# One kernel, two orders of its steps: ScalarE asks for its pair of x first and for b1 last, and Wk's chunks 1 and 0 are turned ahead of the bias

## The chip, the core and the metric

The kernel runs on one core of a Trainium2 chip. The metric is device time in microseconds (us) for one execution, lower is better. The engines are TensorE (PE in the profile; PEld is its weight loads), VectorE (DVE), ScalarE (ACT), GpSimd (POOL) and SyncE (SP), which here only issues DMAs.

## What is computed

`x` is 2048 rows of 448 bf16 values. The output is `x + A(xn) + B(xn)`, with xn the row-normalised x.

```python
def _layernorm(x, axis=-1, eps=1e-5):
    m = jnp.mean(x, axis=axis, keepdims=True); v = jnp.var(x, axis=axis, keepdims=True)
    return (x - m) / jnp.sqrt(v + eps)
...
    # A: linear attention, H = 16 heads of 28
    qkv = (x @ wqkv) ...                       # q, k, v per head
    pq = einsum("bhsd,hdf->bhsf", q, w_phi);  pk = the same of k
    phi_q = concat([softmax(pq), softmax(-pq)]);  phi_k = the same of pk
    kv = einsum("bhsf,bhsd->bhfd", phi_k, v);  z = sum over s of phi_k
    o = einsum(phi_q, kv) / (einsum(phi_q, z) + 1e-6);  A = o @ wo
    # B: a feed-forward block, F = 1792
    h = x @ w1 + b1;  act = h * tanh(softplus(h))     # Mish
    B = act @ w2
```

## The kernel before

The 2048 rows are 16 tiles of 128; two tiles make a unit u (0 to 7). All work is cut into 300 named steps. The string ORDER names each once, and the program calls them in that order (run_order). Each call appends its instructions to the lists of the engines concerned (Program.op); waits are worked out from what each reads and writes. So ORDER sets the order within each engine's list and within each DMA queue, and nothing else: an engine goes through its list in order and waits where an input is late. ORDER also settles the PSUM banks: take1 and take2 hand out the bank or pair of banks (four pairs in all) that has been untouched for longest, at the time of the call. An instruction that opens a bank waits until the bank's last reader is done.

Names in ORDER, with the lines that the profile shows for their instructions. A last letter a, d, p, m or s says which engine does the evacuation or the issue: ScalarE, VectorE, GpSimd, a DMA transpose on SP, or SP.

- Loads. `lx1` to `lx6`: tiles of x (L275); `lkm`, `lvm`, `lkt`: Wk, Wv and their common last 64 rows (L278, L286); `lqT0` to 3: Wq turned by DMA (L290); `l1m0` to 2, `l1t`: W1's chunks and its last rows (L282, L286); `lp`: Wphi (L303); `lb`: b1 (L307); `l2`: W2 (L310); `lo`: Wo (four requests, L317). Those with `a` stand in ScalarE's own list.
- Filler. `zN`: N matmuls of 128x512 on constants (L381), that have no result anyone reads. `table`: ScalarE's table load (L320).
- GpSimd's constants. `pi` (identity and epsilon, L326 to L329), `pm` (mask, L334), `pw` (zeros of Wbd, L343), `pv` (ones beside v, L346), `pp0` to `pp4` (zero columns of buffers, L351), `pk` (mask2 and zeros of KVT, L355 to L364). `bd` makes the block-diagonal Wbd from Wphi (L549).
- Normalisation. `st<t>`: mean and variance of tile t, on VectorE (L472, L473) or on ScalarE (L464 to L468). `rs<u>`: the reciprocal root, on ScalarE (L485, L487), GpSimd (L478, L481) or, with t, ScalarE tile by tile. `xn<u>`: the normalised unit, on VectorE (L506) or GpSimd (L494, L501). `xt<u>`: its transpose, on TensorE with a copy (L514, then L519 on ScalarE or L521 on VectorE), or by DMA (L526).
- Weights of the features. `wtk<c>`: chunk c of Wk turned (L561); `wmk<c>`, `wmq<c>`: its product with Wbd, or that of Wq (L576); each has a copy on L519 or L521. `qd`: a copy within Wq turned (L294). `b1`: b1 turned (L679, copy L521).
- Per unit. `v`, `k`, `q` with u and part 1 or 2: two tiles' matmuls (L443), 8 and 6 of them, and after part 2 a copy of v, or two exponentials of k (L605) or q (L666) on ScalarE. `kn<u>.<s>`: sum and reciprocal on VectorE (L613, L615) and the scaling on GpSimd (L617). `e<t>`: tile t of exp(q) transposed by DMA into EqT (L674). `kv<u>`: the sum over rows (L634); `kvz` takes it to KVZ (L646 on VectorE, then a DMA transpose, L652).
- Feed-forward, first half. `f<q>.<fc>` part 1 and 2: half q of the rows, 128 columns fc of W1 (L443), then Mish on ScalarE into row fc of actT (L685).
- Output. `nd<t>`: numerator and denominator (L708), then six instructions on VectorE (L723 to L734); `ot<u>`: transpose of o by DMA (L743); `G<u>` parts 1 and 2: the second feed-forward product (L848), `g<t>` the same for one tile (L810); `wo<u>`: the product with Wo (L848 or L826). The last of them into a tile is followed by VectorE's addition (L775) and `sto`, `stt`, the store (L866, L863). `wob` copies 64 columns of Wo (L801, L802); `ep` makes a small constant on VectorE (L369, L372).

Buffers are shared. exp(q) of units 3 and 7 lies in row 4 of actT, units 2, 4 and 5 in rows 5, 3 and 2, and units 0, 1 and 6 in Eq0, where turned Wk lies before:

```python
    EQ_ROWS = (None, 4, 5, 3, 2)
    EQ_BUF = (0, 0, 2, 1, 3, 4, 0, 1)
```

Mish of f.4, f.5, f.3 and f.2 therefore waits until the `e` steps have read those rows, and the second user of a buffer waits for the `e` steps of the first. exp(k) of unit u lies in row 8+u.

Of the kernel before, what the change touches and what calls it, by code (L numbers as in the profile page):

```python
# [144 lines left out]


ORDER = """
lpa lx1a lba lvma lx3s lkms lkts lx2s lqT2 lqT1 lqT0 lqT3 lx6s lx0s lx4s table pw pp0 z10 st7d pm st3d st6a l1m1s pi
st2d bd b1 rs3a xn3d wtk2a wtk1a l1m2s wtk0d wmk2a rs1p xt3a pp2 xn1d wmk1a wtk3d wmk0a xt1d st4d wmk3a st5d pp4 v31a
v11d rs2t xn2d st15d v32a v12a k11 qd st14d wmq1a wmq2a xt2d rs7a xn7p wmq3a wmq0d k12 st12d st13d k31 st8d st9d k21 pp1  # L150
rs6p xt7m xn6d rs4p st0d xn4d k32 st11d pk q21 k22 q22 v21a pp3 q11 v22d xt6m ep q31 st10d rs5p xt4m q12 st1d q32 xn5d
rs0a l1m0s v71d pv xn0p k71 v72d xt5m k72 k61 e3 kn3.1 v61a k62 k41 v41a e2 kn2.1 v62a k42 q41 xt0m v42a q42 l1ts q51
v51d kn2.0 kn4.0 q52 e8 e9 kn4.1 kn3.0 q61 v52d q62 k51 e4 e5 kn1.0 kn1.1 kn6.0 k01 k52 kn5.1 f0.11 v01d k02 v02d e12
f1.01 f0.12 f1.31 f1.51 e13 f1.32 f1.02 e10 kn0.0 kn0.1 f1.52 e7 e11 f0.31 q71 f0.21 e6 f0.32 kn7.1 q01 f0.22 f0.131 q02
q72 kv4 kv1 kn6.1 e0 kv3 kv2 kv0 kn5.0 kv6 kv5 kn7.0 kv7 kvz f0.91 e14 f0.132 f1.101 e1 los f1.81 e15 f1.102 f1.82 f1.61
f0.92 wob f1.62 f0.121 nd0 l2a f1.11 f1.21 f1.12 nd1 f0.122 f1.22 f0.51 f0.41 ot0m f0.52 nd3 f1.71 f0.42 f1.72 f0.01
f1.131 nd2 f0.02 f0.61 f1.132 nd4 f0.62 f0.111 f0.81 f0.112 nd5 f0.82 f1.121 f0.101 ot2m nd12 ot1m f0.71 f1.122 f0.72
f0.102 f1.41 f1.111 f1.42 f1.112 nd6 G12 wo21 nd7 G11 nd13 wo11 ot3m f1.91 wo12 G02 nd10 G21 ot6m f1.92 nd11 G01 nd9
wo22 G22 wo61 nd8 G61 ot5m sto2 nd14 G41 G62 ot4m wo62 nd15 G42 wo51 wo31 wo41 wo01 ot7m G51 wo02 sto0 wo32 wo52 G31
wo42 G32 wo7F g14 wo7H G52 stt14 sto4 sto1 sto3 g15 sto5 sto6 stt15  # L160
"""


# [829 lines left out]
```

## Time and profile before

| | us |
|---|---|
| median of 3 runs (152.11 to 154.13) | 153.02 |
| the profiled execution, its own time | 151.93 |
| its span, first to last instruction | 150.2 |
| TensorE busy in it | 145.2 |
| VectorE, ScalarE, GpSimd busy | 101.9, 73.9, 40.4 |

All times of the trace count from the start of the span. A row of the timeline has the start, the duration, the engine (with a q: its sequencer, which issues DMAs and waits), the line of the kernel, the operation, what is written and read, the count of merged instructions and, in brackets, how long the engine sat idle before it and what ended that. The table by stretch gives each engine's busy time in each, then the granted clock of TensorE, the DMA share and GB/s. A row of a line's instructions gives count and shortest, median and longest duration in ns. The chain of waits gives start, length and what the end of the kernel was waiting for. A matmul's duration includes its way through the array, so that neighbours overlap; the steps from start to start show the rate.

### The profile page before, as it was taken

The numbers are of one execution on the slowest core, as the hardware profiler recorded it, in microseconds if no ns is written. First come the engines' busy times: TensorE is split into PE (matmuls) and PEld (weight loads), VectorE is DVE, ScalarE is ACT, GpSimd is POOL, SyncE is SP. The second block draws the span as 40 slices with busy tenths as digits, with TensorE's granted clock in tenths as the row PEclk, the third lists the DMA queues.
The fourth block names the chain that finished last, engine by engine and source line by source line (L and its number), as shares of the span: only waits on it lengthen the run. The fifth ranks groups of instructions, "written<-read, shape, count | busy, mean of one in ns | idle before, by whom it ended". The sixth has DMA issues, their size and how long they took to land.

```text
span 150.2 us, 4003 instructions
## 1 busy us (share of the span) xinstructions
PE 145.2 (97%) x1736; PEld 76.0 (51%) x1736; DVE 101.9 (68%) x227; ACT 73.9 (49%) x93; POOL 40.4 (27%) x58
## 2 busy tenths in 40 slices
PE   7799999999999999999979999999999999999993
PEld 2485555455544485454435445545555555554552
DVE  0788998999999803069759966897899755025231
ACT  2887999999899499848286485000200000000000
POOL 5330674599999990000000000000000000000000
PEclk9999999999999999999999999999999999999999
DMA  5999258496999904989900060033031300210054
GB/s 128 310 186 373 115 105 190 97 183 153 159 188 189 143 0 86 193 244 274 270 0 0 4 122 0 4 61 65 2 61 65 61 4 15 46 65 0 0 214 153
DMA packets 39069, 17.01 MB, mean 113 GB/s; under 512 B 33036, under 2 KB 38284, under 8 KB 39052
## 3 DMA queue, kind: packets, MB, share of 16 engines
q1 hardware_dynamic: 36064, 14.46, 43.6%
q10 hardware_dynamic: 2988, 2.31, 5.4%
q8 instruction: 13, 0.21, 0.6%
q14 instruction: 4, 0.03, 0.1%
HBM read 7.02 MB, written 1.84 MB: 59 GB/s over the span
## 4 chain that ended last, share of the span: by engine, by line
PE 71%; DMA 13%; ACT 6%; SPq 6%; issue 1%; ACTq 1%; DVE 0%
PE PS L848 31%; PE PS L443 30%; DMA EqT<-actT 10%; SPq L674 5%; PE PS L810 3%; DMA b_rows<-in_B_b_dram 3%; PE PS L708 2%; ACT actT L685 2%; SPq L317 1%; PE PS L576 1%; PE PS L561 1%; ACT Eq L666 1%; ACT actT L666 1%; PE PS L514 1%; PE PS L826 1%
## 5 line engine op out<-in xcount | busy, mean ns | idle before, releaser
L443 PE MATMUL PS<-xnT,W 64*128 64x512 bf16 x392 | 44.7, 376 | 0.0
L685 ACT ACTIVATE actT<-PS,b1T 128x1024 bf16<-128x1024 f32 x28 | 29.9, 1112 | 26.7 <-PE PS L443 23.1
L848 PE MATMUL PS<-W,actT 64*128 64x448 bf16 x392 | 39.2, 349 | 0.0
L443 PEld LDWEIGHTS PS<-xnT,W 64*128 64x128 bf16 x392 | 18.2, 94 | 21.5 <-ACT actT L685 0.9
L848 PEld LDWEIGHTS PS<-W,actT 64*128 64x128 bf16 x392 | 18.6, 94 | 16.6
L617 POOL TENSOR_TENSOR actT<-actT,rSk 128x896 bf16<-128x896 bf16 x16 | 26.5, 1701 | 0.6 <-DVE rSk L615 0.6
L775 DVE TENSOR_TENSOR x_all<-PS,x_all 128x448 bf16<-128x448 f32 (+1 forms) x16 | 9.3, 615 | 18.4 <-PE PS L848 14.2
L613 DVE TENSOR_REDUCE Sk<-actT 128x32 f32<-128x896 bf16 x16 | 16.6, 1040 | 0.1
L605 ACT ACTIVATE actT<-PS 128x896 bf16<-128x896 f32 x16 | 13.6, 916 | 0.9 <-PE PS L443 0.9
L443 PE MATMUL PS<-Wkv,xnT 64*128 64x448 bf16 x112 | 12.6, 349 | 0.0
L443 PE MATMUL PS<-Wpq,xnT 64*128 64x448 bf16 x112 | 12.4, 349 | 0.0
L472 DVE BATCH_NORM_STATS2 stats<-x_all 128x6 f32<-128x448 bf16 x15 | 9.1, 610 | 4.6 <-DMA x_all<-in_A_x_dram 4.6
L723 DVE COPY Sq<-PS 128x16 f32<-128x16 f32 x32 | 4.0, 167 | 12.1 <-PE PS L708 12.1
L443 PE MATMUL PS<-Wpk,xnT 64*128 64x448 bf16 x112 | 12.1, 349 | 0.0
L734 DVE TENSOR_TENSOR xn<-v_all,rden 128x448 bf16<-128x448 f32 x16 | 10.0, 625 | 1.3 <-DMA Wkv<-xn 0.8
L731 DVE TENSOR_TENSOR v_all<-v_all 128x464 f32<-128x464 f32 x16 | 10.3, 642 | 0.6
L727 DVE TENSOR_TENSOR v_all<-PS,Sq 128x464 f32<-128x464 f32 x16 | 10.3, 641 | 0.5
L729 DVE TENSOR_TENSOR v_all<-PS,Sq 128x464 f32<-128x464 f32 x16 | 10.1, 630 | 0.0
L666 ACT ACTIVATE actT<-PS 128x896 bf16<-128x896 f32 x10 | 8.6, 950 | 0.0
L443 PEld LDWEIGHTS PS<-Wpq,xnT 64*128 64x128 bf16 x112 | 5.4, 94 | 5.3
L708 PEld LDWEIGHTS PS<-KVZ,EqT 56*128 56x128 bf16 x256 | 5.7, 93 | 4.5 <-ACT actT L685 1.3
L443 PEld LDWEIGHTS PS<-Wkv,xnT 64*128 64x128 bf16 x112 | 5.4, 94 | 5.1
(88 smaller groups left out, 131.3 us busy)
## 6 DMA issues: line engine op xcount, KB each, us to landing
W<-in_B_w_dram ACTq DMA_DIRECT2D x1, 1568.0 KB, 10.8
out_dram<-x_all SPq DMA_DIRECT2D x7, 224.0 KB, 2.2
W<-in_B_w_dram SPq DMA_DIRECT2D x3, 448.0 KB, 5.5
x_all<-in_A_x_dram SPq DMA_DIRECT2D x2, 448.0 KB, 4.4
x_all<-in_A_x_dram SPq DMA_DIRECT2D x3, 224.0 KB, 4.0
Wo<-in_A_wo_dram SPq DMA_DIRECT2D x2, 336.0 KB, 4.7
W<-in_B_w_dram SPq DMA_DIRECT2D x2, 224.0 KB, 3.7
Wkv<-in_A_wqkv_dram SPq DMA_DIRECT2D x1, 336.0 KB, 4.6
```

Source lines behind the costliest of these rows:

```text
L443: ins = e.matmul(o, lhs(c, k), rhs(c, k), start=part == "1" and c == 0, stop=part == "2" and c == 2)
L605: op("ACT", lambda e, s=s: e.activation(E_of(u)[:, s, :, :], two(b, D), ACT.Exp, scale=1.0 if s == 0 else -1.0), r=[pb(b), pb(b + 1)], w=[ ...
L613: op("DVE", lambda e: e.tensor_reduce(Sk[u][:, s, :], Eh(), AX.X, ALU.add), r=[("E", u, s)], w=[("Sk", u, s)], tag=f"Sk{u}.{s}")
L617: op("POOL", lambda e: e.tensor_tensor(Eh(), Eh(), ap_on(rSk[u][:, s, 0:1], [[1, 2 * H], [0, DH]]), ALU.mult), r=[("E", u, s), ("rSk", u, ...
L666: op("ACT", lambda e, s=s: e.activation(Eq_of(u)[:, :, s, :].rearrange("p i (h n) -> p i h n", n=64)[:, :, :, 0:QP], two(b, D).rearrange(" ...
L685: op("ACT", lambda e: e.activation(actT[:, fc, q * 1024:(q + 1) * 1024], bank(b, 2), ACT.Mish, bias=b1T[:, fc:fc + 1]), r=[("b1T",), pb(b) ...
L727: op("DVE", lambda e: e.tensor_tensor(tv(t1[i]), num(0), sx(1), ALU.mult), r=[pb(b), pb(b + 1), ("Sq", i, 1)], w=[("t1", i)], tag=f"ta{t}")
L729: op("DVE", lambda e: e.tensor_tensor(tv(t2), num(1), sx(0), ALU.mult), r=[pb(b), pb(b + 1), ("Sq", i, 0)], w=[("t2",)], tag=f"tb{t}")
L731: op("DVE", lambda e: e.tensor_tensor(t1[i], t1[i], t2, ALU.add), r=[("t1", i), ("t2",)], w=[("t1", i)], tag=f"tc{t}")
L734: op("DVE", lambda e: e.tensor_tensor(o_sb[(t // 2) % 2][:, t % 2, :].rearrange("p (h d) -> p h d", d=DH), t1[i][:, :, 0:DH], ap_on(rden[i ...
L775: op("DVE", lambda e: e.tensor_tensor(x_all[:, t, 0:n], bank(b)[:, 0:n], x_all[:, t, 0:n], ALU.add), r=[pb(b), ("x", t)], w=[("out", t)], ...
L848: ins = e.matmul(bank(places[par][0])[:, 0:D], l, r, start=fresh[par], stop=places[par][2] and i >= len(todo) - 2)
```

## The change

Only ORDER changes: the same 300 places are filled anew. Of the steps, z10 becomes z14, Wo's loads move from SP's queue to ScalarE's, and these change their engine: rs1 (GpSimd to ScalarE), rs2 (ScalarE, tile by tile, to both tiles at once), rs7 (ScalarE to GpSimd), xn7 (GpSimd to VectorE), the copies of xt3, wmk0, wmk3 and v4 (ScalarE to VectorE), and those of xt1, wtk0, wtk3 and wmq0 (VectorE to ScalarE). A v step's letter counts in part 2 only; the first parts whose letter changes do the same as before. Of the two lists:

```diff
-lpa lx1a lba lvma lx3s lkms lkts lx2s lqT2 lqT1 lqT0 lqT3 lx6s lx0s lx4s table pw pp0 z10 st7d pm st3d st6a l1m1s pi
-st2d bd b1 rs3a xn3d wtk2a wtk1a l1m2s wtk0d wmk2a rs1p xt3a pp2 xn1d wmk1a wtk3d wmk0a xt1d st4d wmk3a st5d pp4 v31a
+lx1a lpa lvma lba lx3s lkms lkts lx2s lqT2 lqT1 lqT0 lqT3 lx6s lx0s lx4s st7d pk table z14 pi st2d st6a rs3a st3d rs1a
+pv pp0 xn3d xn1d wtk1a wtk0a b1 wtk2a l1m1s pm xt3d pw wtk3a st5d bd wmk0d st4d xt1a wmk1a wmk2a wmk3d rs2a pp2 v31d
...
-v51d kn2.0 kn4.0 q52 e8 e9 kn4.1 kn3.0 q61 v52d q62 k51 e4 e5 kn1.0 kn1.1 kn6.0 k01 k52 kn5.1 f0.11 v01d k02 v02d e12
+l1ts q51 l1m2s kn4.0 q42 e6 v51a q52 kn2.1 v52d kn7.1 kn4.1 e9 q61 k51 q62 k52 k01 v01a e10 kn3.1 kn7.0 f1.01 k02 e5
+v02d f1.02 kn3.0 f1.51 f0.11 kn5.0 f1.31 kn0.0 f0.12 e8 f1.52 e11 e13 e7 f1.32 f0.21 q71 kn2.0 f0.22 ep q72 kn5.1 q01
+f1.131 e12 e15 f0.31 kn0.1 q02 f0.32 kv3 e14 kv2 kv5 kv1 kv4 kv6 kv7 kv0 kvz f1.11 f1.101 f1.132 f1.12 f1.102 f0.121
...
-q72 kv4 kv1 kn6.1 e0 kv3 kv2 kv0 kn5.0 kv6 kv5 kn7.0 kv7 kvz f0.91 e14 f0.132 f1.101 e1 los f1.81 e15 f1.102 f1.82 f1.61
-f0.92 wob f1.62 f0.121 nd0 l2a f1.11 f1.21 f1.12 nd1 f0.122 f1.22 f0.51 f0.41 ot0m f0.52 nd3 f1.71 f0.42 f1.72 f0.01
+f0.52 nd1 ot0m f0.92 l2a f0.71 f0.01 f0.81 f0.02 nd4 f0.82 f0.72 f0.111 nd3 f1.111 f1.121 ot1m f1.112 f0.112 f1.81 nd5
+f1.122 f1.82 f1.91 nd7 loa nd6 f1.92 wob ot2m G12 G31 nd13 G11 f1.41 ot3m nd12 wo11 wo31 f1.42 wo32 nd11 G32 ot6m G61
...
-wo42 G32 wo7F g14 wo7H G52 stt14 sto4 sto1 sto3 g15 sto5 sto6 stt15
+sto1 wo7F wo22 G52 ot4m wo7H stt14 wo41 G22 sto5 wo42 sto2 g15 sto4 stt15
```

Engine by engine: ScalarE asks for x1, Wphi, Wv, b1 in place of Wphi, x1, b1, Wv. GpSimd begins with pk, pi, pv, pp0, pm, pw, bd in place of pw, pp0, pm, pi, bd. TensorE's small steps after the filler are wtk1, wtk0, b1, wtk2, xt3, wtk3, wmk0, xt1, wmk1, wmk2, wmk3 in place of b1, wtk2, wtk1, wtk0, wmk2, xt3, wmk1, wtk3, wmk0, xt1, wmk3. On SP, W1's chunk 2 (l1m2) moves from behind chunk 1 to behind l1t, and the e steps go 3 2 4 6 9 10 5 8 11 13 7 12 15 14 (kvz) 1 0 in place of 3 2 8 9 4 5 12 13 10 7 11 6 0 (kvz) 14 1 15.

More of the change, by code (lines that the diff above doesn't have):

```diff
@@ L147 @@
 ORDER = """
-lpa lx1a lba lvma lx3s lkms lkts lx2s lqT2 lqT1 lqT0 lqT3 lx6s lx0s lx4s table pw pp0 z10 st7d pm st3d st6a l1m1s pi
-st2d bd b1 rs3a xn3d wtk2a wtk1a l1m2s wtk0d wmk2a rs1p xt3a pp2 xn1d wmk1a wtk3d wmk0a xt1d st4d wmk3a st5d pp4 v31a
-v11d rs2t xn2d st15d v32a v12a k11 qd st14d wmq1a wmq2a xt2d rs7a xn7p wmq3a wmq0d k12 st12d st13d k31 st8d st9d k21 pp1
-rs6p xt7m xn6d rs4p st0d xn4d k32 st11d pk q21 k22 q22 v21a pp3 q11 v22d xt6m ep q31 st10d rs5p xt4m q12 st1d q32 xn5d
-rs0a l1m0s v71d pv xn0p k71 v72d xt5m k72 k61 e3 kn3.1 v61a k62 k41 v41a e2 kn2.1 v62a k42 q41 xt0m v42a q42 l1ts q51
@@ L153 @@
-v51d kn2.0 kn4.0 q52 e8 e9 kn4.1 kn3.0 q61 v52d q62 k51 e4 e5 kn1.0 kn1.1 kn6.0 k01 k52 kn5.1 f0.11 v01d k02 v02d e12
-f1.01 f0.12 f1.31 f1.51 e13 f1.32 f1.02 e10 kn0.0 kn0.1 f1.52 e7 e11 f0.31 q71 f0.21 e6 f0.32 kn7.1 q01 f0.22 f0.131 q02
-q72 kv4 kv1 kn6.1 e0 kv3 kv2 kv0 kn5.0 kv6 kv5 kn7.0 kv7 kvz f0.91 e14 f0.132 f1.101 e1 los f1.81 e15 f1.102 f1.82 f1.61
-f0.92 wob f1.62 f0.121 nd0 l2a f1.11 f1.21 f1.12 nd1 f0.122 f1.22 f0.51 f0.41 ot0m f0.52 nd3 f1.71 f0.42 f1.72 f0.01
-f1.131 nd2 f0.02 f0.61 f1.132 nd4 f0.62 f0.111 f0.81 f0.112 nd5 f0.82 f1.121 f0.101 ot2m nd12 ot1m f0.71 f1.122 f0.72
@@ L158 @@
-f0.102 f1.41 f1.111 f1.42 f1.112 nd6 G12 wo21 nd7 G11 nd13 wo11 ot3m f1.91 wo12 G02 nd10 G21 ot6m f1.92 nd11 G01 nd9
-wo22 G22 wo61 nd8 G61 ot5m sto2 nd14 G41 G62 ot4m wo62 nd15 G42 wo51 wo31 wo41 wo01 ot7m G51 wo02 sto0 wo32 wo52 G31
-wo42 G32 wo7F g14 wo7H G52 stt14 sto4 sto1 sto3 g15 sto5 sto6 stt15
+lx1a lpa lvma lba lx3s lkms lkts lx2s lqT2 lqT1 lqT0 lqT3 lx6s lx0s lx4s st7d pk table z14 pi st2d st6a rs3a st3d rs1a
+pv pp0 xn3d xn1d wtk1a wtk0a b1 wtk2a l1m1s pm xt3d pw wtk3a st5d bd wmk0d st4d xt1a wmk1a wmk2a wmk3d rs2a pp2 v31d
@@ new lines @@
+v11a xn2d v32a v12a k11 pp3 st14d qd wmq2a wmq0a st15d xt2d wmq1a st12d wmq3a k12 k21 q21 pp1 rs7p k22 q11 q22 xn7d
+st13d q12 xt7m st8d rs6p st9d xn6d v21a rs4p st10d xn4d l1m0s k31 v22d st11d st1d xt6m q31 k32 q32 st0d xt4m e3 rs5p
+v71a rs0a xn5d xt5m e2 k71 v72d k72 k61 xn0p pp4 v61d kn1.0 k62 v41a k41 kn1.1 kn6.0 xt0m v62a kn6.1 e4 k42 v42d q41
+l1ts q51 l1m2s kn4.0 q42 e6 v51a q52 kn2.1 v52d kn7.1 kn4.1 e9 q61 k51 q62 k52 k01 v01a e10 kn3.1 kn7.0 f1.01 k02 e5
+v02d f1.02 kn3.0 f1.51 f0.11 kn5.0 f1.31 kn0.0 f0.12 e8 f1.52 e11 e13 e7 f1.32 f0.21 q71 kn2.0 f0.22 ep q72 kn5.1 q01
@@ new lines @@
+f1.131 e12 e15 f0.31 kn0.1 q02 f0.32 kv3 e14 kv2 kv5 kv1 kv4 kv6 kv7 kv0 kvz f1.11 f1.101 f1.132 f1.12 f1.102 f0.121
+f0.101 f0.131 f0.122 f0.102 f0.132 f1.21 e1 f0.61 f1.22 f1.61 f0.62 e0 nd2 f0.41 f1.62 nd0 f1.71 f0.42 f0.51 f1.72 f0.91
+f0.52 nd1 ot0m f0.92 l2a f0.71 f0.01 f0.81 f0.02 nd4 f0.82 f0.72 f0.111 nd3 f1.111 f1.121 ot1m f1.112 f0.112 f1.81 nd5
+f1.122 f1.82 f1.91 nd7 loa nd6 f1.92 wob ot2m G12 G31 nd13 G11 f1.41 ot3m nd12 wo11 wo31 f1.42 wo32 nd11 G32 ot6m G61
+nd10 ot5m G02 sto3 nd8 wo12 G01 wo01 wo61 nd9 G21 wo02 G62 wo62 sto6 nd15 G41 wo52 wo21 nd14 ot7m wo51 G51 G42 g14 sto0
```

## The prediction, written before the changed kernel was run

> **What bounds the kernel now.** I read the page's busy times first, then the busy time by stretch.
>
> ```profile
> span 150.2 us, 4003 instructions
> ...
> PE 145.2 (97%) x1736; PEld 76.0 (51%) x1736; DVE 101.9 (68%) x227; ACT 73.9 (49%) x93; POOL 40.4 (27%) x58
> ```
>
> ```profile
> core 0: us, PE busy (x) PEld busy (x) DVE busy (x) ACT busy (x) POOL busy (x), PEclk, DMA share, GB/s
> ...
> 5.28:6.18 0.90, 0.00 (x0) 0.03 (x1) 0.68 (x2) 0.87 (x3) 0.00 (x0) 1.00 1.02 234
> 6.18:10.57 4.39, 4.38 (x47) 4.21 (x48) 3.70 (x13) 3.50 (x8) 1.58 (x4) 1.00 1.01 216
> 10.57:75.28 64.71, 64.71 (x791) 33.33 (x789) 49.58 (x104) 53.62 (x68) 35.79 (x39) 1.00 0.80 175
> 75.28:76.27 0.99, 0.18 (x2) 0.00 (x1) 0.00 (x0) 0.99 (x2) 0.00 (x0) 1.00 0.00 0
> 76.27:147.25 70.98, 70.98 (x879) 36.71 (x880) 46.41 (x107) 12.66 (x12) 0.00 (x0) 1.00 0.18 44
> ```
>
> TensorE is the bound from 10.57 to 147.25 us: it is full there but for one hole at 75.28. The change keeps every matmul of that stretch, so an order can win only in the head (before 10.57), in that hole, and in the tail of 2.96 us after 147.25. It loses wherever a feeder of TensorE becomes late. Next, the head on TensorE's timeline:
>
> ```profile
> 0.85 4.43 PE L381 MATMUL PS<-const-bfloat16-1.0 128*128 128x512 bf16 x10 [0.85 <-PEq L978]
> 6.18 0.17 PE L679 MATMUL PS<-ident,b_rows 14*128 14x14 bf16 x1 [0.91 <-DMA b_rows<-in_B_b_dram]
> ...
> 8.00 0.95 PE L514 MATMUL PS<-ident,xn 128*128 128x128 bf16 x7
> ...
> 9.86 0.56 PE L514 MATMUL PS<-ident,xn 128*128 128x128 bf16 x7
> ...
> 10.57 2.82 PE L443 MATMUL PS<-Wkv,xnT 64*128 64x448 bf16 x28
> ```
>
> Ten filler matmuls (z10) end at 5.28; TensorE then idles 0.91 us until b1 lands; then the 15 small steps run (turns of Wk and x, products for Wpk) until v3's first matmul at 10.57. The same seven transposes take 0.95 us at 8.00 and 0.56 us at 9.86: TensorE runs at half rate until about 9.7, although PEclk says 1.00. Its 4.43 us of filler did not lift that; the 3.5 unbroken us from 6.18 did. So the head is slow because the filler was followed by an idle gap.
>
> **The head.** The first two requests of ScalarE's queue, x1 and Wphi, swap; b1 goes behind Wv. z10 becomes z14, and b1 goes from first to third of the small steps. The rows of the steps that I use:
>
> ```profile
> 1.80 4.25 DMA b_rows<-in_B_b_dram
> ...
> 5.97 0.29 ACT L485 ACTIVATE lnv<-mv,eps_col 128x2 f32<-128x2 f32 x1
> 6.30 0.20 ACT L487 ACTIVATE rstd<-lnv 128x2 f32<-128x2 f32 x1
> ...
> 9.80 1.42 ACT L519 ACTIVATE Wpk<-PS 128x448 bf16<-128x448 f32 x3
> ```
>
> ```profile
> 5.47 0.63 DVE L472 BATCH_NORM_STATS2 stats<-x_all 128x6 f32<-128x448 bf16 x1 [0.87 <-DMA x_all<-in_A_x_dram]
> ...
> 6.23 0.59 DVE L472 BATCH_NORM_STATS2 stats<-x_all 128x6 f32<-128x448 bf16 x1
> ...
> 7.01 0.88 DVE L506 TENSOR_SCALAR xn<-x_all,mv,rstd 128x448 bf16<-128x448 bf16 x3
> ...
> 8.32 1.10 DVE L506 TENSOR_SCALAR xn<-x_all,mv,rstd 128x448 bf16<-128x448 bf16 x3
> ...
> 10.45 0.63 DVE L521 COPY xnT<-PS 128x896 bf16<-128x896 bf16 x1 [0.24 <-PE PS L514]
> ```
>
> z14 at z10's rate is 14/10 x 4.43 = 6.2 us, so filler stands from 0.85 to at most 7.05 and covers what was idle. x1 is requested where Wphi was, 0.4 us earlier, so VectorE's two statistics (0.76 us apart) end at about 6.5 in place of 6.95. rs3 ends at 6.50 as now; rs1 moves from GpSimd to ScalarE and takes 0.5 more, to 7.0. xn3 runs 6.5 to 7.4, xn1 behind it to 8.3; now xn1 ends at 9.4. ScalarE's four copies of turned Wk at 0.5 each then run from about 7.2 to 9.2, and the last wmk and v3 can follow: v3's first matmul at about 9.7, where it was 10.57, **a gain of 0.9**. This asks for TensorE at full rate. The other bound: the 15 steps cost the 4.39 us that they cost now and start at 7.05, so v3 starts at 11.4, a loss of 0.9. I take the gain: after 3.5 unbroken us from 6.18 TensorE ran fast, and now its work is unbroken from 0.85 on.
>
> b1 is issued 0.4 us later and queues behind Wv's 336 KB. At its 4.25 us it lands at 6.5, before the third step at about 7.3: nothing. If it lands a us later, TensorE waits some 0.5 us, part of it under the wait for xn3.
>
> The Trainium skill, "TensorE: Matmul & The Clock Gate", Part 4, says that transposes do not count as work that lifts the gate. This trace speaks against it: most of the 3.5 us from 6.18 were transposes, and the rate doubled. By the rule a gate still shut at 7.05 stays shut until v3; that is the rival below. Part 1 says that the window of about 3.4 us runs freely, so that the moment varies between executions; one profile cannot show that.
>
> **GpSimd in the head** now makes mask2 first. Its rows:
>
> ```profile
> 20.87 0.15 POOL L355 MEMSET mask<- 128x56 f32 x1
> ...
> 22.34 0.53 POOL L364 MEMSET KVT<- 128x512 uint32 x1
> ...
> 25.94 0.55 POOL L346 MEMSET v_all<- 128x256 uint32 x1
> ```
>
> ```profile
> 4.03 1.08 POOL L549 TENSOR_TENSOR Wbd<-Wraw,mask 112x224 bf16<-112x224 bf16 x2 [1.09 <-DMA Wraw<-in_A_w_phi_dram]
> ```
>
> mask2 takes 2.0 us and the ones 0.55 us, so the identity is ready 2 us later (about 3.6; needed at 5.8) and Wbd at about 6.6, where it was 5.1; its first use is at about 8.3. Nothing, with 1.7 us to spare.
>
> **The middle.** From v3 to the first kv TensorE has the same 43.2 us of work. Its feeders:
>
> ```profile
> 28.47 1.08 DVE L613 TENSOR_REDUCE Sk<-actT 128x32 f32<-128x896 bf16 x1
> ...
> 43.16 1.03 DVE L521 CAST v_all<-PS 128x896 bf16<-128x896 f32 x1
> ```
>
> ```profile
> 30.02 26.55 POOL L617 TENSOR_TENSOR actT<-actT,rSk 128x896 bf16<-128x896 bf16 x16 [0.61 <-DVE rSk L615]
> ```
>
> ```profile
> 39.22 1.03 PE L443 MATMUL PS<-xnT,W 64*128 64x512 bf16 x8
> ...
> 53.78 3.42 PE L634 MATMUL PS<-actT,v_all 128*60 128x112 bf16 x128
> ```
>
> GpSimd's 26.55 us chain ends at 56.57, just ahead of kv's end at 57.2: TensorE cannot come out of kv earlier unless this chain starts earlier. It will: VectorE reaches it about 1.5 us sooner, since xn1 is done 1 us sooner, ep (0.4) moves behind, and two waits on reciprocals go; against this xn7 (0.9) comes to VectorE, for a Wpq copy (0.6) that leaves it. v4's copy (1.03) comes to VectorE behind four sums, too, so v0's copy ends at about 43.2 to 44, where it ended at 44.2; TensorE asks for its banks at 43.6 (v3's 9.7, and 43.2 less the 9.3 us of steps that stand between that place and kv: three q parts of 0.6 to 0.8, the f parts at 0.65 and 0.86). I count 0.1 here, 0.1 for Wpq's copies and 0.1 for kv's bank, which waits for q7's second exponential almost to the tenth: **0.3 lost**, bounds 0 and 1.5.
>
> W1's last chunk moves from before xt7 in SP's queue to behind xt0, e4 and the tail:
>
> ```profile
> L282 SPq DMA_DIRECT2D W<-in_B_w_dram x3: 433/433/578, 10.3 to 23.4; - x3
> ...
> DMA to landing us min/median/max: 3.6/4.5/6.1
> ```
>
> xn0 ends before GpSimd's chain begins (28.6 then); xt0, e4 and the two tail requests hold the queue for some 1.3, 1.3 and 1.2 us, so the issue is near 33 and the landing at 36.6 to 39.1. The first f step stands at 39.22 now; it moves 0.9 us forward with v3 and 0.76 back behind a v part, to 39.1. Nothing, but here the cover is thin.
>
> **The hole at 75.28.** The chain of waits and the issues round it:
>
> ```profile
> 65.07 9.96 DMA EqT<-actT
> ...
> 76.27 0.39 PE PS L708 x16
> ```
>
> ```profile
> 62.70 2.32 SPq L317 DMA_DIRECT2D Wo<-in_A_wo_dram  x4
> 65.07 2.63 SPq L674 DMA_TRANSPOSE EqT<-actT  x1
> ```
>
> ```profile
> W<-in_B_w_dram ACTq DMA_DIRECT2D x1, 1568.0 KB, 10.8
> ...
> EqT<-actT SPq DMA_TRANSPOSE x10, 3.3
> ```
>
> e15 reads row 4 of actT, which f0.4's Mish overwrites. It stands behind the four requests for Wo on SP and beside W2's 1568 KB, and takes 9.96 us where the median is 3.3. ScalarE waits, and the nd step at 76.27 finds no bank: the hole of 0.99 us above, 0.81 of it idle. In the new order e15 and e14 go ahead of kvz (near 53 us), W2 is requested after f0.92, Wo after f1.82 on ScalarE's queue. e15 lands 10 us before f0.4's Mish. **Gain 1.0**; the bounds are 0 (another wait takes its place) and 1.1. What is late next: W2, issued about 13 us of TensorE work ahead of G1 (10.8 to land), and Wo, with 11 us until wo1 against 6.7 for its slowest request now; both fit.
>
> The tail keeps its form (g15, two additions, two stores of t15): nothing.
>
> **Sum.** The profiled execution took 151.93 us, its span of 150.2 and 1.7 around it: 151.93 - 0.9 - 1.0 + 0.3 = **150.3**. It is the fastest of the runs shown, whose median is 153.02; against that the forecast is 1.8% less.
>
> **Rivals.** (1) The head gives nothing: TensorE is at half rate until 11.4 and the hole still closes: 151.93 + 0.9 - 1.0 + 0.3 = 152.1. For it: 4.43 us of filler lifted nothing. Against: 3.5 unbroken us did. (2) A new wait takes the hole's place, a VectorE copy of v0 or an nd bank, at 1.5 us in place of 0.3: 151.5. For it: VectorE is 35 of 38 us busy in the middle. (3) Slower: W1's last chunk. SP's queue is in order, and this request now stands behind xt0, which waits for GpSimd's xn0. From a landing past 39.1 each us is one of TensorE; past 41.8 it ends slower than the median before. Issued at 38 with 6.1 to land it is 44.1, 5.0 lost: 155.3. Against it: even now GpSimd is past xn0 at 30.02, so that the issue would have to be 5 us late. (4) The skill's rule on transposes, where the filler's end finds the gate shut: v3 at 11.4, and 3.5 us more at half rate from there, 1.7 lost: 152.1 + 1.7 = 153.8. (5) The change does not do what it says: z14 ends at 7.05 but Wk lands late too, or the order of ScalarE's two first requests leaves x1 where it was, since all loads share the same engines (1.02 busy there): the head gives 0.3, 150.9.
>
> **How the numbers follow.** Forecast 0.56, (1) 0.10, (2) 0.15, (3) 0.05, (4) 0.04, (5) 0.10. The forecast's own range is 149.2 to 151.1, from a head that gains 0.4 to 1.7 and small waits of 0 to 0.6. 8 in 10 take in (5), (2) and (1): 149.2 to 152.5. 2% is 3.1 us, about what a measurement tells from no change: faster is below 149.96, half of the forecast's own weight: 0.28; slower is above 156.1, only the far end of (3) and (4): 0.03; the rest 0.69.
>
> **What would show it.** Right: no idle between filler and turns; seven transposes at 0.56 us from the first; v3 at 9.7; GpSimd's chain from about 28.6; no TensorE idle near 75; e15 landing in 3.3. Wrong: transposes still at 0.95, a TensorE wait on W1 near 39 or on an addition's or copy's bank in the middle, or on W2 before G1.

## The result, and the profile after

The changed kernel took 157.08 us (median of 4, 155.46 to 157.69), where the kernel before took 153.09 beside it: a ratio of 1.027 (1.0225 to 1.032), slower. The forecast was 150.3 us, and its range ended at 152.5. Ratios, here and below, leave out executions over 1.5% above the fastest of their kernel, which medians and ranges keep; one of 537 us, of the kernel with all four mends below (TensorE busy for 531.7), is in no range and no reading.

The profiled execution took 157.69 us (151.93 before). Its page:

```profile
span 155.9 us, 4011 instructions
...
PE 145.9 (94%) x1740; PEld 76.6 (49%) x1740; DVE 107.1 (69%) x229; ACT 73.4 (47%) x91; POOL 38.4 (25%) x55
```

TensorE's busy time is that of before, its span 5.7 us longer: TensorE waits more. VectorE is busy 5.2 us longer with almost the same instructions, so some of these must have been held. Next, the busy time by stretch, cut at TensorE's own events:

```profile
7.00:10.30 3.30, 0.00 (x1) 0.01 (x1) 2.82 (x6) 1.44 (x5) 1.51 (x5) 1.00 1.26 235
10.30:13.90 3.60, 3.60 (x39) 3.41 (x40) 2.67 (x7) 2.21 (x4) 0.00 (x0) 0.60 1.02 326
13.90:57.60 43.70, 43.58 (x452) 21.82 (x451) 40.80 (x78) 38.77 (x51) 28.97 (x26) 0.99 0.79 142
57.60:62.15 4.55, 3.55 (x132) 3.23 (x130) 1.53 (x3) 4.06 (x5) 3.44 (x3) 1.00 0.62 119
62.15:90.40 28.25, 28.25 (x336) 13.17 (x332) 13.09 (x31) 17.43 (x17) 0.00 (x0) 1.00 0.39 95
90.40:92.00 1.60, 0.35 (x6) 0.11 (x4) 1.53 (x6) 1.60 (x2) 0.00 (x0) 1.00 0.00 0
92.00:152.50 60.50, 60.50 (x755) 32.21 (x754) 41.73 (x95) 4.51 (x5) 0.24 (x1) 1.00 0.31 66
```

Three holes stand there: 3.3 us in the head, 1.0 inside kv (57.60 to 62.15), and one near 90.4 that keeps 1.25 idle. The hole at 75.28 is gone: from 62.15 to 90.40 TensorE is full. Stage by stage against before: v3's first matmul 10.57 to 13.90 is +3.3; from there to the first kv 43.2 to 43.8 is +0.6; kv 3.4 to 4.5 is +1.1; from kv's end to TensorE's last matmul 90.1 to 90.4 is +0.3 (1.0 won at the old hole, 1.3 lost at the new one); the tail 3.0 to 3.3 is +0.3. Together, before rounding, 5.7.

The chain that ended last names who was late at each:

```profile
2.32 7.93 DMA b_rows<-in_B_b_dram
...
52.91 3.54 DVE epsT L372
56.45 1.01 DVE Sk L613
...
57.91 1.71 POOL actT L617
...
84.30 5.43 DMA Wkv<-xn
89.82 0.63 DVE xn L734
```

b1 came 7.93 us after its issue (4.25 before). An instruction on one column, ep's last, held VectorE for 3.54 us, and a sum, a reciprocal and GpSimd's scaling behind it were late for kv. The transpose of o of unit 0 (ot0, landing in a free part of Wkv's buffer) took 5.43. The same three on TensorE's timeline:

```profile
0.85 4.83 PE L381 MATMUL PS<-const-bfloat16-1.0 128*128 128x512 bf16 x14 [0.85 <-PEq L978]
6.37 0.62 PE L561 MATMUL PS<-ident,Wkv 128*112 128x128 bf16 x8 [0.69 <-DMA Wkv<-in_A_wqkv_dram]
10.30 0.18 PE L679 MATMUL PS<-ident,b_rows 14*128 14x14 bf16 x1 [3.30 <-DMA b_rows<-in_B_b_dram]
...
11.90 0.95 PE L514 MATMUL PS<-ident,xn 128*128 128x128 bf16 x7
...
59.66 2.55 PE L634 MATMUL PS<-actT,v_all 128*60 128x112 bf16 x96 [1.00 <-POOL actT L617]
...
91.90 1.04 PE L443 MATMUL PS<-xnT,W 64*128 64x512 bf16 x8 [1.25 <-DVE v_all L729]
```

The filler did its work: 14 of its matmuls took 4.83 us where 10 took 4.43. But after 3.3 idle us the seven transposes are at 0.95 again, and PEclk of that stretch is 0.60.

What VectorE and GpSimd did beside it (VectorE's timeline, then GpSimd's):

```profile
7.11 2.82 DVE L506 TENSOR_SCALAR xn<-x_all,mv,rstd 128x448 bf16<-128x448 bf16 x6 [0.56 <-ACT rstd L487]
```

```profile
6.68 1.08 POOL L549 TENSOR_TENSOR Wbd<-Wraw,mask 112x224 bf16<-112x224 bf16 x2 [1.43 <-DMA Wraw<-in_A_w_phi_dram]
...
33.20 23.23 POOL L617 TENSOR_TENSOR actT<-actT,rSk 128x896 bf16<-128x896 bf16 x14
57.91 3.35 POOL L617 TENSOR_TENSOR actT<-actT,rSk 128x896 bf16<-128x896 bf16 x2 [1.48 <-DVE rSk L615]
```

xn3 and xn1 are three pieces each, which took 0.88 and 1.10 us before; here all six take 2.82. The first of them, 1.52 us of that (0.39 before), stands beside GpSimd's Wbd and the three memsets behind it. ep's 3.54 us, from 52.91 to 56.45, lie inside GpSimd's unbroken 23.23 and end with it, at 56.43: the instruction got through when GpSimd itself had nothing left. Last, the DMA issues of ScalarE in the head (KB each, us to landing):

```profile
Wkv<-in_A_wqkv_dram ACTq DMA_DIRECT2D x1, 336.0 KB, 8.1
...
Wraw<-in_A_w_phi_dram ACTq DMA_DIRECT2D x1, 24.5 KB, 5.2
```

Wv, issued at 1.76, landed at 9.9, and b1's step began at 10.30. b1 itself was there at 10.25. Wphi, now asked second, took 5.2 where it took 3.1.

### The profile page after: what moved, and what is told of

It reads as the page before. It is cut to its first block, busy times and chain, and to the rows that moved or that the text cites. A ratio compares the mean times of both kernels' runs of the same rounds, so it can differ in the third digit from the quotient of the medians.

```text
span 155.9 us, 4011 instructions
## 1 busy us (share of the span) xinstructions
PE 145.9 (94%) x1740; PEld 76.6 (49%) x1740; DVE 107.1 (69%) x229; ACT 73.4 (47%) x91; POOL 38.4 (25%) x55
## 4 chain that ended last, share of the span: by engine, by line
PE 65%; DVE 19%; DMA 9%; ACT 2%; issue 1%; POOL 1%; ACTq 1%; DVEq 0%
PE PS L848 30%; PE PS L443 25%; DVE Sk L613 9%; DMA b_rows<-in_B_b_dram 5%; DMA Wkv<-xn 3%; DVE rSk L615 3%; PE PS L810 3%; DVE epsT L372 2%; PE PS L708 2%; DVE v_all L521 2%; PE PS L634 2%; PE PS L576 2%; POOL actT L617 1%; ACT actT L666 1%; PE PS L514 1%
## 5 line engine op out<-in xcount | busy, mean ns | idle before, releaser
L443 PE MATMUL PS<-Wpk,xnT 64*128 64x448 bf16 x112 | 12.7, 349 | 0.0
```

Source lines behind the costliest of these rows:

```text
L443: ins = e.matmul(o, lhs(c, k), rhs(c, k), start=part == "1" and c == 0, stop=part == "2" and c == 2)
```

## The experiments

**Theory**: three separate losses stand on top of the forecast's gains: (A) b1 behind Wv in ScalarE's queue, with TensorE waiting in order behind b1's step; (B) ep beside GpSimd's chain; (C) W2's request just ahead of ot0's transpose. **Rivals**: for A, the head is slow by the new order of the turns, whatever b1 does; for B, the sums are late by the order of the middle, and ep only stands where the wait shows; for C, the bank of nd3 is late by the order of the nd steps.

### b1 asked for ahead of Wv

```diff
-lx1a lpa lvma lba lx3s
+lx1a lpa lba lvma lx3s
```

> The changed order with one edit: b1's request stands ahead of Wv's in ScalarE's queue again (third, not fourth). Theory A (b1's few bytes wait behind Wv's 336 KB in one queue, and TensorE, which takes its steps in order, stands still at the third small step until b1 is there): b1 lands near 7, TensorE does not idle for more than 0.5 us there, v3's first matmul comes at 9.7 to 10.6 in place of 13.9, and the time falls by 3.3 to 4 us from 157.08, to about 153.3. Rival B (all loads are slow at the start because the 16 engines are full, so b1 lands at 10 from any place): no change, 156.5 to 157.5.

154.11 us (154.02 to 154.50), ratio 1.0117 (1.0086 to 1.0148). TensorE's timeline:

```profile
7.13 0.18 PE L679 MATMUL PS<-ident,b_rows 14*128 14x14 bf16 x1
...
8.65 0.56 PE L514 MATMUL PS<-ident,xn 128*128 128x128 bf16 x7 [0.98 <-DVE xn L506]
...
10.55 2.93 PE L443 MATMUL PS<-Wkv,xnT 64*128 64x448 bf16 x28
```

One swap of two requests gives back more than half: 1.0273 to 1.0117 is 2.4 us of 153, of 4.2; 3.3 to 4 were expected. v3 stands at 10.55. Transposes run at 0.56 throughout, so the order of the turns is not what made the head slow. What is left there is 0.98 us of wait for xn3.

### b1 turned later

The step moves behind wmq0a; its request stays behind Wv.

```diff
-wtk1a wtk0a b1 wtk2a l1m1s
+wtk1a wtk0a wtk2a l1m1s
...
-wmq2a wmq0a st15d
+wmq2a wmq0a b1 st15d
```

> The changed order with one edit: b1's request stays last in ScalarE's queue, but TensorE turns it behind wmq0, some 13 us into the kernel, when it has long landed. Theory A: b1 lands at about 10 as now, nobody waits for it, and the time falls as in the run with b1 ahead of Wv, to about 153.3; v3 cannot start ahead of Wv's landing, 9.9 in the changed kernel. Rival B (the small steps are late for another cause, such as Wbd or the copies): v3 stays near 13 and the time near 157.

155.18 us (155.03 to 155.34), ratio 1.0185 (1.0149 to 1.0221): 1.3 us back. v3 starts at 10.70 and nothing waits for b1, whose step is at 14.73. So A is b1's place on TensorE together with its late landing. The expected 153.3 was missed: the median is 1.1 us above that of the swapped requests. The two profiled executions (155.03 and 154.50) are only 0.5 apart, of which 0.15 shows at v3, 0.2 on the way to kv, 0.15 inside kv and 0.1 behind it; the rest isn't settled.

### The old kernel with b1 behind Wv

```diff
-lpa lx1a lba lvma lx3s
+lpa lx1a lvma lba lx3s
```

> The kernel before with one edit: b1's request goes behind Wv's, to the last place in ScalarE's queue. There b1 is the first of the small steps. Theory A: TensorE idles from 5.3 to about 10, all small steps move behind it, and the time rises by 3.5 to 4.5 us, to about 157. Rival B: b1 lands where it did, at 6, and the time stays near 153.

156.76 us (155.38 to 157.69), ratio 1.0278 (1.0207 to 1.0349): this one part alone costs the old order as much as the whole change.

```profile
8.99 0.17 PE L679 MATMUL PS<-ident,b_rows 14*128 14x14 bf16 x1 [4.26 <-DMA b_rows<-in_B_b_dram]
...
10.80 0.95 PE L514 MATMUL PS<-ident,xn 128*128 128x128 bf16 x7
...
13.98 2.19 PE L443 MATMUL PS<-Wkv,xnT 64*128 64x448 bf16 x20
```

b1's step moves from 6.18 to 8.99. Both groups of seven transposes take 0.95, and v3 is at 13.98: 3.4 us later, though b1 is only 2.8 later.

### ep early

```diff
-st10d xn4d l1m0s
+st10d xn4d ep l1m0s
...
-f0.22 ep q72
+f0.22 q72
```

> The changed order with one edit: ep, three small VectorE instructions, moves from between the last sums of k back to behind xn4, where GpSimd's chain of scalings has not begun. Theory C (ep's last instruction reads two SBUF operands and cannot run while GpSimd's chain runs back to back; it takes 3.54 us in place of 0.16, the sums behind it are late, GpSimd then stands idle for 1.5 us and kv for 1.0): ep takes 0.5 us in all, GpSimd's chain runs through, kv has no hole, and the time falls by 1.0 to 1.5 us to about 155.8. Rival D (the chain of GpSimd is the bound of kv whatever VectorE does): kv still ends near 62 and the time stays within 0.4 of 157.

155.32 us (154.40 to 157.40), ratio 1.0171 (1.0101 to 1.024). ep's last instruction, now at 23.0, takes 0.16 us, and kv is unbroken from 55.18 to 58.45. So the order of the middle has no other late sum: loss B is ep. This profile shows one more thing, on TensorE's timeline and in the stretch behind b1:

```profile
9.36 0.18 PE L679 MATMUL PS<-ident,b_rows 14*128 14x14 bf16 x1 [2.74 <-DMA b_rows<-in_B_b_dram]
...
9.74 0.55 PE L514 MATMUL PS<-ident,xn 128*128 128x128 bf16 x7
```

```profile
9.36:11.63 2.27, 2.27 (x39) 2.16 (x40) 1.61 (x6) 1.67 (x3) 0.00 (x0) 1.00 0.93 205
```

The same 39 matmuls took 2.27 us at a granted 1.00 here, after 2.74 idle us, and 3.60 at 0.60 in the changed kernel, after 3.30. So a late b1 costs its wait and, in some executions, 1.3 us more by the clock. The changed kernel's own executions fit that: three with a mean granted clock of 0.989 took 156.9 to 157.7 us, the one with 1.000 took 155.5.

### ep in its late place, with another instruction

ep's last instruction reads two columns as tensors. `tensor_scalar` takes the second as a scalar of each partition and computes the same.

```diff
-        op("DVE", lambda e: e.scalar_tensor_tensor(epsT[:, 2:3], epsT[:, 0:1], DEN_EPS / 2, epsT[:, 1:2], ALU.mult,
-                                                   ALU.add), r=[("epsT", 0), ("epsT", 1)], w=[("epsT", 2)], tag="ep2")
+        op("DVE", lambda e: e.tensor_scalar(epsT[:, 2:3], epsT[:, 0:1], DEN_EPS / 2, epsT[:, 1:2], op0=ALU.mult,
+                                            op1=ALU.add), r=[("epsT", 0), ("epsT", 1)], w=[("epsT", 2)], tag="ep2")
```

> The changed order with ep at its late place, and its last instruction written with one tensor operand and a per-partition scalar in place of two tensor operands (same result). Theory C1 (two SBUF tensor operands need the path that GpSimd's chain holds): it takes 0.2 us or less, GpSimd's chain has no gap, kv no hole, and the time falls as in the run with ep early, to about 155.5. Rival C2 (any small fp32 VectorE instruction between SBUF and SBUF there is held up, whatever its operands): it still takes 3.5 us and the time stays near 157.

155.95 us (154.91 to 157.26), ratio 1.0191 (1.0127 to 1.0254). The profiled execution is the slowest of its four, 157.26. VectorE's timeline, then TensorE's:

```profile
53.37 0.21 DVE L372 TENSOR_SCALAR epsT<-epsT 128x1 f32<-128x1 f32 x1
```

```profile
9.57 0.19 PE L679 MATMUL PS<-ident,b_rows 14*128 14x14 bf16 x1 [2.89 <-DMA b_rows<-in_B_b_dram]
...
10.15 0.95 PE L514 MATMUL PS<-ident,xn 128*128 128x128 bf16 x7
...
58.15 3.34 PE L634 MATMUL PS<-actT,v_all 128*60 128x112 bf16 x128
```

In the same place, beside the same GpSimd chain, it takes 0.21 us in place of 3.54, and kv is whole. So B is not the late place as such, but this instruction with two tensors from SBUF beside GpSimd. (The operation changed together with its operands; no run separates the two.) This is what the Trainium skill says, "SBUF — State Buffer", section "Who interferes with whom", that a VectorE instruction with two SBUF inputs contends with a GpSimd instruction that reads SBUF, and in the summary of that page, that the one issued second blocks until the first is finished. The trace agrees, and adds that one instruction is not the most it can cost: GpSimd's chain of 14 in 23.23 us is 1.66 for each, and ep's 3.54 is more than two of them. In the head, two rows show one thing more: after 2.89 idle us the transposes are at half rate at once.

### ep late in the old kernel

```diff
-xt6m ep q31
+xt6m q31
...
-kn7.1 q01
+kn7.1 ep q01
```

> The kernel before with one edit: ep moves from its early place to between the last sums of k, where GpSimd's chain of scalings runs. Theory C: ep's last instruction takes 2 to 4 us in place of 0.16, GpSimd's chain gets a gap, kv a hole, and the time rises by 0.5 to 1.5 us. Rival D: no change, since VectorE is idle for 5 us behind the sums in that kernel and GpSimd's chain has the inputs ahead of time.

152.95 us (151.83 to 154.93), ratio 1.0011 (0.9973 to 1.0048): no cost, where theory C had 0.5 to 1.5. ep is held for 1.60 us and kv stays whole:

```profile
48.58 1.60 DVE L372 SCALAR_TENSOR_TENSOR epsT<-epsT 128x1 f32<-128x1 f32 x1
```

```profile
54.02 3.41 PE L634 MATMUL PS<-actT,v_all 128*60 128x112 bf16 x128
```

The hold is half as long there, and three sums still follow it, so GpSimd's chain does not run dry. In the changed kernel two sums follow, and GpSimd waits 1.48 for the first. A hold alone costs nothing; it costs where the chain behind it catches up.

### b1 and ep together, then W2 as well

First both mends; then also W2's request 22 us earlier, just behind kv (59.65; it was at 81.83).

```diff
-f1.101 f1.132 f1.12
+f1.101 f1.132 l2a f1.12
...
-ot0m f0.92 l2a f0.71
+ot0m f0.92 f0.71
```

> The changed order with b1 ahead of Wv and ep early, W2 where the change has it. The two causes add up if they lie on one chain of TensorE's work: 157.08 - 3.0 (measured for b1 alone) - 1.1 to 1.8 (ep alone) = 152.3 to 153.0, with the hole of some 1.9 us near 87 still there. If instead ep's cost only showed because b1 had already made all late, the time is that of b1 alone, 154.1.

> The changed order with three edits: b1 ahead of Wv, ep early (the two of the runs before), and W2 asked for behind f1.13's Mish, some 20 us earlier. Theory E (the hole of 1.3 to 1.7 us near 87 to 90 comes because ot0's transpose, in flight together with W2, needs 5.4 us; nd4's last product waits for ot0 to have read the buffer, nd3 is queued behind it on VectorE, and f1.8 waits for nd3's bank): ot0 lands in about 3 us, the hole is gone, and with 154.1 less 1.2 for ep the time is 152.9 - 1.6 = 151.3. Rival F (ot0 is issued too late for nd4 whatever W2 does): ot0 takes 3 us but a hole of over 0.8 us stays, and the time is 152.2 or more.

Both mends: 152.93 us (152.63 to 153.53), ratio 1.0013 (0.9977 to 1.0049); v3 10.01, kv whole, and a hole of 1.58 at 87.04 is left, again for an nd bank. With W2 early: **151.17 us** (151.03 to 151.20), ratio 0.990 (0.9855 to 0.994), 1.0% below the kernel before. Its head on TensorE, and the DMA issues from 57 to 82 us:

```profile
8.07 0.56 PE L514 MATMUL PS<-ident,xn 128*128 128x128 bf16 x7 [0.74 <-DVE xn L506]
...
10.03 2.94 PE L443 MATMUL PS<-Wkv,xnT 64*128 64x448 bf16 x28
```

```profile
W<-in_B_w_dram ACTq DMA_DIRECT2D x1, 1568.0 KB, 10.0
...
Wkv<-xn SPq DMA_TRANSPOSE x1, 2.9
```

ot0 lands in 2.9 in place of 5.4, and no hole is left behind kv. By the ratios the three mends give 2.4, 1.6 and 1.7 us one after the other.

### W2 early alone

> The changed order with W2 asked for behind f1.13's Mish and nothing else. Theory E (W2 beside ot0's transpose makes the hole near 90): ot0 takes about 3 us to land, the hole of 1.6 us goes, and the time falls by 1.2 to 1.6 us to about 155.6. Rival F (the hole is that of a VectorE that began its nd work 5 us late): a hole of over 0.8 us stays and the time is above 156.4.

155.47 us (154.31 to 155.87), ratio 1.0156 (1.0086 to 1.0227): 1.8 us back, as above. The DMA issues from 80 to 93 us, then TensorE:

```profile
Wkv<-xn SPq DMA_TRANSPOSE x2, 2.9
```

```profile
9.92 0.18 PE L679 MATMUL PS<-ident,b_rows 14*128 14x14 bf16 x1 [2.64 <-DMA b_rows<-in_B_b_dram]
...
10.29 0.55 PE L514 MATMUL PS<-ident,xn 128*128 128x128 bf16 x7
...
11.11 0.78 PE L514 MATMUL PS<-ident,xn 128*128 128x128 bf16 x7
11.68 1.32 PE L576 MATMUL PS<-Wbd,Eq 112*128 112x112 bf16 x12
...
59.28 2.55 PE L634 MATMUL PS<-actT,v_all 128*60 128x112 bf16 x96 [0.85 <-POOL actT L617]
```

ot0 is back at 2.9 and the third hole is gone, with the nd steps where the change put them; b1's and ep's losses stay. Loss C is W2 beside ot0. In the head the seven transposes run at 0.55 right behind b1, the next seven take 0.78, and the twelve products 1.32 (0.76 at full rate): the rate fell 1.3 us after the work was taken up again.

### The filler alone in the old kernel

```diff
-table pw pp0 z10 st7d
+table pw pp0 z14 st7d
```

> The kernel before with one edit: z10 becomes z14. Theory G (filler without a gap lets TensorE run at full rate before the small steps; it was the head's gain that was forecast): the filler's last matmuls come 0.22 us apart, the small steps start at about 6.2 at full rate, v3 starts at 9.6 to 10.2 where it was 10.57, and the time falls by 0.4 to 1 us. Rival H (the small steps wait for copies and statistics, not for TensorE): v3 stays at 10.4 to 10.6 and the time within 0.3 us.

151.94 us (151.42 to 155.29), ratio 0.995 (0.9906 to 0.9994). TensorE's timeline:

```profile
6.46 0.18 PE L679 MATMUL PS<-ident,b_rows 14*128 14x14 bf16 x1
...
8.04 0.56 PE L514 MATMUL PS<-ident,xn 128*128 128x128 bf16 x7
...
10.25 2.82 PE L443 MATMUL PS<-Wkv,xnT 64*128 64x448 bf16 x28
```

Unbroken filler to 6.5 lets the small steps run at full rate; v3 comes 0.3 earlier, at 10.25, between what the theory (10.2 at most) and the rival (10.4 at least) allow. In the old order the full rate is worth no more, since the steps begin 0.3 later and then wait for xn1 (0.33) and a copy of Wk (0.24).

### All four: Wphi first as well

The kernel with three mends, with Wphi asked first again and GpSimd's zeros and mask2 in an order that leaves Wbd unhindered; the memsets pp1 to pp3 go behind rs7 as well (not among the lines here).

```diff
-lx1a lpa lba lvma lx3s
+lpa lx1a lba lvma lx3s
...
-st7d pk table z14 pi st2d
+st7d pi pm pw pp0 pk table z14 st2d
...
-l1m1s pm xt3d pw wtk3a st5d bd wmk0d
+l1m1s xt3d bd pv wtk3a st5d wmk0d
```

> The changed order with b1 ahead of Wv, ep early and W2 early, and a fourth edit: Wphi is asked for first again, ahead of x1, GpSimd makes Wbd right behind mask2, and its three buffer memsets pp1 to pp3 go behind rs7. Theory I (VectorE's first xn3 instruction, 1.5 us in the changed kernel against 0.39 before, is held up while GpSimd runs Wbd and the memsets without a gap): xn3's first instruction takes 0.4 to 0.6 us, both pairs are normalised by 8.5, v3 starts at 9.6 or sooner where it was 10.03, and the time falls by 0.4 to 0.8 us from 151.2, to about 150.6. Rival J (what moves v3 is the landing of x and Wk, which Wphi ahead of x1 makes later): xn3 starts later by what it gains, v3 stays near 10.0 and the time at 151.2.

> The same kernel as the run with all four edits, for a profile that can be read. Theory I (xn3's first instruction is held only because GpSimd makes Wbd late): that instruction takes about 0.37 us, TensorE does not wait for xn3 any more, v3's first matmul stands at about 9.4 in place of 10.03, and the half microsecond that is won is lost again further on, in the middle. Rival I2: with Wphi's request first, x1 and Wk land later by about what the hold gave back (Wk near 6.6 in place of 6.2), the wait moves from xn3 to the turn of Wk, and v3 stays between 9.9 and 10.2. The time is about 151.2 by both.

151.35 us (150.74 to 152.05), ratio 0.990 (0.9869 to 0.9932), and 151.62 in the one profiled again: the same as with three mends. TensorE's timeline, then VectorE's:

```profile
6.71 0.62 PE L561 MATMUL PS<-ident,Wkv 128*112 128x128 bf16 x8 [1.18 <-DMA Wkv<-in_A_wqkv_dram]
...
8.48 0.56 PE L514 MATMUL PS<-ident,xn 128*128 128x128 bf16 x7 [0.68 <-DVE xn L506]
...
10.60 2.82 PE L443 MATMUL PS<-Wkv,xnT 64*128 64x448 bf16 x28
```

```profile
6.08 0.63 DVE L472 BATCH_NORM_STATS2 stats<-x_all 128x6 f32<-128x448 bf16 x1 [1.46 <-DMA x_all<-in_A_x_dram]
...
7.56 1.66 DVE L506 TENSOR_SCALAR xn<-x_all,mv,rstd 128x448 bf16<-128x448 bf16 x6
```

The hold on xn is gone (six pieces in 1.66; 2.23 with three mends, 2.82 in the changed kernel). But x1, asked second, arrives at 6.08, and VectorE takes its statistics ahead of xn3. TensorE waits 1.18 for Wk and still 0.68 for xn3, so v3 comes 0.6 later than with three mends. My theory for this run, that the hold was the head's last loss, falls; the rival holds in kind, and even its 9.9 to 10.2 was too early. What the swap of x1 and Wphi gives on one side it takes on the other.

## Why the prediction was wrong

**The head's rate: right.** Unbroken work does lift TensorE's rate: the transposes take 0.56 from the first in the old kernel with z14 and wherever z14 stands and b1 is on time. But in the old order that moved v3 by only 0.3, so the gap behind the filler was a small part of why that head was slow. The expected end of the filler, at most 7.05, was 5.68, so Wk's landing left 0.7 us idle.

**"b1 is issued 0.4 us later and queues behind Wv's 336 KB. At its 4.25 us it lands at 6.5 ... nothing": this step failed.** The 4.25 was measured with b1 ahead of Wv, and I carried it to a place behind Wv. b1 took 7.93 and TensorE idled 3.3 us, with the clock shut behind it. Putting the request back gave 2.4 us; the late b1 alone cost the old kernel 4.1 (156.76 against 152.68). The second bound, "if it lands a us later, TensorE waits some 0.5", was no bound: the nearest row was Wv's own transfer of 336 KB, behind which b1 cannot come early. In the five profiles in which TensorE waits for b1 behind Wv, b1 landed 0.2 to 0.5 us after it (9.86 and 10.25 in the changed kernel). The Trainium skill, "DMA: Bandwidth & Descriptors", section "Queues, rings and completion order", says that each DMA engine takes the descriptors of a ring in order, though a later one may finish first; the traces agree with the order. Why Wv itself took 6.8 to 8.1 ahead of b1, and 5.1 to 6.4 behind it, no run shows.

**GpSimd's head, "nothing, 1.7 us to spare": wrong in kind.** TensorE never waited for Wbd. Wbd was late by Wphi and not by mask2: the swap of the first two requests was priced for x1 alone, and GpSimd waited 1.43 us for Wphi. What it delayed is VectorE's xn3, for which TensorE waited 0.98 once b1 was on time. The first piece of xn3 took 0.60 to 1.52 us in the eight profiles where Wbd runs beside it, and 0.37 to 0.39 in the five others. "rs3 ends at 6.50 as now" failed too: it ended at 7.08, since b1's request took ScalarE 1.11 us to issue (0.69 before) and ScalarE's steps behind it moved back. But no order that I ran won that time back: Wphi first delays x1 and Wk.

**The middle, 0.3 lost: 1.7 lost.** "ep moves behind" was counted as a gain for VectorE. It was 3.54 us of VectorE and 1.0 to 1.2 of kv, since the instruction that took 0.16 with GpSimd idle stands still beside GpSimd's chain. The rest is the 0.6 up to kv: by the steps from start to start, 0.25 of it is matmuls still at half rate behind 13.9, and 0.27 a step at 43.83 that waits for ScalarE to have read a bank (its exponential of q). W1's thin cover held: TensorE waited for no transfer of W1.

**The hole at 75: right, and "What is late next: W2 ... both fit" wrong.** The 1.0 was won. W2 itself was in time. I asked only whether it lands before G1, and not what else moves while it does: ot0 takes 5.4 beside it, where it takes 2.9 without, and the next nd steps' bank was late with it, for 1.3 to 1.6 us. This is rival (2), an nd bank in the hole's place, near its 1.5, with a chance of 0.15; but it came on top of A and B, which no rival held. Rival (1), half rate up to v3, had the rate but not the idle time ahead of it, and of rival (5) only the late Wk came. Rivals (3) and (4) did not occur; the half rate that did come back was from idling and not from transposes.

**The tail, nothing: 0.3 lost.** It lies behind the landing of the last store: from there to the end it is 0.81 us, where it was 0.47. The profiles of the old orders have 0.47, those of the changed one 0.80 or 0.81, but for the one with all four edits (0.46). Why, no run shows.

With A, B and C taken back, the profiled execution is 151.14, 0.8 above the forecast: the head gives 0.5 (v3 at 10.03) in place of 0.9, the stretch behind kv 0.8 in place of 1.0 (1.1 up to TensorE's last matmul, less the tail's 0.3), and the one up to kv (10.03 to 53.78) loses 0.5 in place of 0.3.

## What to carry to other kernels

A landing time belongs to a place in a queue: when a small request moves behind a large one, its price is the large one's landing, and an engine that works in order pays all of it. Ask of each moved instruction what runs beside it in the new place, and of each moved load what other transfers it will slow, not only whether it is in time itself. And judge a reordering by its parts: here three losses, each with a cause of its own, hid a gain of 1%.

## What the runs showed of the hardware

- After idle time TensorE's rate fell back at no fixed moment: at once after 3.30 us (39 matmuls in 3.60 us, PEclk 0.60) and after 2.89 (seven transposes in 0.95), 1.3 us after the end of a wait of 2.64, and not at all after 2.74 (2.27 us, PEclk 1.00). Ahead of the waits of 3.30 and 2.64 stood another, for Wk, of 0.69 and 0.84 with 0.6 us of work between; the 2.89 had none. The Trainium skill, "TensorE: Matmul & The Clock Gate", Part 1, has a window of about 3.4 us that runs freely and a gate that falls back after an idle one; the changing moment fits the free run, and the 2.89 shows that a wait shorter than the window can cost the rate too.
- ep's instruction on 128x1 elements took 0.16, 1.60 or 3.54 us, by what GpSimd was doing. What let it in after one GpSimd instruction in the old kernel, and only at the end of the chain in the changed one, no run shows.
- A DMA transpose (ot0) that landed in 2.9 us in three profiles took 5.4 to 5.8 in the six in which a load of 1568 KB was requested 2.5 us ahead of it.
